# Attention before a mixture of experts: q, k and v in another layout in DRAM, and no transposes of q and k

## The chip, the cores and the metric

One core of one Trainium2 chip runs the whole program. The metric is the device time of one execution in microseconds (us); lower is better.

## The reference

Attention over 4 batches, 8 heads, 768 tokens and a head dimension of 64, in float32, and after it a mixture of 8 experts on the 3072 rows of 512 that it gives. A token sees the first 8 tokens and those up to 95 before it.

```python
scores = scale * np.matmul(q, k.transpose(0, 1, 3, 2))
keep = is_global | is_local            # global: pos < 8; local: 0 <= rel < 96
scores = np.where(keep, scores + bias, -1000000000.0)
a = np.exp(scores - np.max(scores, axis=-1, keepdims=True))
out = np.matmul(a / (np.sum(a, axis=-1, keepdims=True) + 1e-09), v)
x = out.transpose(0, 2, 1, 3).reshape(B * S, H * D)
...
logits = x @ w_gate
expert_idx = np.argmax(logits, axis=1)      # each token to one expert, by order of arrival
h = np.maximum(np.einsum('ecd,edf->ecf', disp, w1), 0.0)
y = np.einsum('ecf,efd->ecd', h, w2)
out[i] = gate_w[i] * y[expert_idx[i], pos[i]]
```

## The kernel before

The kernel has two stages. Attention (`banded`, line 560) goes through 24 blocks of 128 tokens, six to a batch; each block has two units of four heads, so there are 48 units. Behind it come the expert layers (from line 1042), 8 experts with 3 products of split float32 each.

A block goes through these steps, which the plan's jobs name:

- `load` (line 610): SyncE issues three DMAs, of q, k and v, each [128 tokens, 8 heads x 64] with one piece of 64 floats for each token and head.
- `turn` (line 648): 16 transposes on TensorE put the four head pairs of k and of q with the head dimension on rows into a pair of PSUM banks; `keep_qk` (line 658) copies them into the tile `K`, one half by VectorE, one by ScalarE (helper `keep_half`, line 194). A tile `K` serves two blocks and has two buffers.
- `keep_window` (line 666), once for two blocks, on GpSimd: copies of the last 96 keys of the block before and of the 8 global keys into the new tile.
- `scores` (line 687): 16 products for one unit, from the tile `K`. `maximum` (line 679) on VectorE adds the bias and takes the maximum, `exponential` (line 710) on ScalarE, `transpose_p` (line 727) on TensorE, `keep_p` (line 741) copies on VectorE and ScalarE, `weigh` (line 748) multiplies by v on TensorE. Three tiles `probs` hold the units' scores in turn.
- `load_window` (line 643): SyncE copies the last 96 rows of the block before from its tile `nat_v` in SBUF to a tile beside it; `load_globals` and `spread_globals` (lines 635 and 640) do so with the first 8 rows, once a batch.
- `keep_x`, `turn_x`, `scale_x`, `write_x`: the block's rows are turned back, scaled and written to DRAM (`xrows`). For every three blocks the routing steps (`zm` to `g`) and `write_slots` follow; some of them run on GpSimd.

Beside this, SyncE loads 12 pieces of 256 KB of the first expert's weights (job `weights`, tile `wst`, line 251), and GpSimd splits each into a high and a low part (`cast` at line 267, `split` at line 262).

The order of the work of all five engines in this stage is written out beforehand: the class `Plan` runs through the jobs with a cost each, and at each free moment of an engine takes the ready job with the least sum of its block number and its kind's number in `RANK`. The instructions are issued in that order; each engine, and SyncE's queue, works strictly in it. The setup of the bias (line 567) and the first loads stand ahead of the plan. `setup` makes `bias0` on VectorE (line 601) and `bias1` on GpSimd (line 603).

Of the kernel before, what the change touches and what calls it, by code (L numbers as in the profile page):

```python
# [12 lines left out]
F32 = mybir.dt.float32  # L13
# [9 lines left out]
P = 128  # L23
NEG = -1.0e9
FIXED = 4
FIRST = 2


class Plan:


    LATENCY = {"PE": 0.2, "ACT": 0.06, "DVE": 0.06, "POOL": 0.1, "SP": 2.1}
# [67 lines left out]
    def run(self, rank):  # L100
        for _, n in self.order(rank):
# [5 lines left out]
RANK = dict(landed=-8.58, load=-2.25, window=-0.06, globals=-0.01, spread=-0.22, turn=0.87, keep_qk=-1.73,  # L107
            keep_window=1.18, scores=-1.56, maximum=-0.47, exp=2.58, transpose_p=2.10, keep_p=1.46, weigh=3.45, sums=1.68,
            turn_sums=3.79, keep_x=2.05, turn_x=2.13, scale_x=2.07, write_x=2.06, zm=-1.83, za=2.95, lt=-0.50, ll=-0.09,
            m=0.12, f=3.81, np=-0.00, ne=5.82, nc=3.06, p=1.07, k=3.23, s=3.57, g=0.71, at=2.57, write_slots=-2.15,  # L110
            weights=1.88, cast=8.05, split=17.96, numbers=3.75, early=17.34, first=18.21, was_late=20.67,
            fetch_early=24.58, start_rows=19.45, turn_first=21.93, keep_high=22.50, keep_low=21.76, layer1_first=25.47,
            find_late=20.56, name_late=19.99, fetch_late=19.72)
# [3 lines left out]
def fused(ctx: ExitStack, tc, q, k, v, wg, w1, w2, out, n_global, n_local, cap):  # L117
    nc = tc.nc
    B, H, S, D = q.shape
# [7 lines left out]
    PREV, G = 96, 8  # L127
# [326 lines left out]
    def numbers(after=None):  # L454
        slot_i = small.tile([P, T4], I32, name="slot_i", bufs=1)
# [104 lines left out]
    def banded():  # L560
# [6 lines left out]
        def setup():  # L567

            rel_i = nat.tile([P, P], I32, name="rel_i", bufs=1)
            nc.gpsimd.iota(rel_i, pattern=[[-1, P]], base=0, channel_multiplier=1)  # L570
            rel0 = nat.tile([P, P], F32, name="rel0", bufs=1)
            nc.vector.tensor_copy(rel0, rel_i)
            rel1 = nat.tile([P, W], F32, name="rel1", bufs=1)
# [22 lines left out]
            near = nat.tile([P, HW], F32, name="near", bufs=1)  # L596
# [13 lines left out]
        def load(i, which="qkv"):  # L610

            b, j = blocks[i]
            d = st_[i]
            for n, src in zip("qkv", (q, k, v)):
                if n not in which:
                    continue
                d[n] = nat.tile([P, H * D], F32, name="nat_" + n, bufs=5 if n == "v" else 3)
                nc.sync.dma_start(out=d[n].rearrange("p (h d) -> p h d", h=H),  # L618
                                  in_=src[b, :, j * P:(j + 1) * P, :].rearrange("h p d -> p h d"))

        for which in ("qk", "v"):
            for i in range(2):
                load(i, which)
        setup()
        kpool = actx.enter_context(tc.tile_pool(name="kpool", bufs=2))
# [3 lines left out]
        probs = [soft.tile([P, HP + 4 * (HW + HP)], F32, name="sc", bufs=3) for _ in range(3)]  # L629
        for t in probs:  # L630
            nc.gpsimd.memset(t[:, 0:HP], 0.0)
            nc.gpsimd.memset(t[:, HP:].rearrange("p (a x) -> p a x", a=4)[:, :, HW:], 0.0)
        beside = [vpool.tile([PREV + G, H * D], F32, name="v1", bufs=3) for _ in range(3)]

        def load_globals(i):

            first["vg"] = vpool.tile([G, H * D], F32, name="vg")
            nc.sync.dma_start(out=first["vg"], in_=st_[i]["v"][0:G])

        def spread_globals(n):  # L640
            nc.sync.dma_start(out=beside[n][PREV:PREV + G], in_=first["vg"])

        def load_window(i):

            st_[i]["v1"] = beside[i % 3]
# [137 lines left out]
        for r in range(2):  # L783
            keep_qk(0, r)
# [640 lines left out]
```

## Time and profile before

| | us |
|---|---|
| median of 3 runs | 510.45 |
| lowest, highest | 509.27, 514.66 |
| the profiled execution | 513.04 |
| its span, first to last instruction | 511.2 |

The profile shows one execution. PE stands for TensorE's products, PEld for its loads of weights, DVE for VectorE, ACT for ScalarE, POOL for GpSimd, SP for SyncE, SPq for the issues on its queue. Products overlap each other on PE, so its busy time is that of their union, with ends that are modelled. The chain of work that ended last is followed back from the last instruction, at each step to what released it. A wait is put down to what came last of all that was waited for. Times on POOL are rough.

### The profile page before, as it was taken

To read this page: it belongs to the slowest core of one execution; us is meant where nothing else is said; L and a number is where in the kernel's file an instruction comes from. 1 tells how busy PE (TensorE), PEld (TensorE's weight loads), DVE (VectorE), ACT (ScalarE), POOL (GpSimd) and SP (SyncE) were. 2 spreads that over 40 slices of the span, in tenths; PEclk is the share of its full clock that TensorE was granted. 3 is DMA by queue.
4 is the path that set the end of the run, shared out by engine and by line. 5 is a ranking of instruction groups with operands and counts; after the bars stand their busy time and mean duration, and the time that the engine had idled before them with its cause. 6 is when DMAs were issued, how large, how long until landed. Compare 5 with 4: busy or idle time off the path is not lost.

```text
span 511.2 us, 12541 instructions
## 1 busy us (share of the span) xinstructions
PE 460.5 (90%) x4495; PEld 381.6 (75%) x4495; DVE 299.2 (59%) x925; ACT 295.0 (58%) x810; POOL 145.6 (28%) x265
## 2 busy tenths in 40 slices
PE   7799979878799779997999999999999999999780
PEld 4678757666577668786988999988989888988560
DVE  6588868767678652642664655645655554655430
ACT  4699877877797513343545555545555545555440
POOL 6022326654665412330311312121223103003011
PEclk9799999999998979998999999999999999999995
DMA  9899797879984317891653664554555355322001
GB/s 177 175 241 220 163 215 151 212 187 226 209 215 134 85 33 150 289 351 37 216 179 85 228 189 149 163 168 118 200 188 184 111 169 180 98 87 107 9 5 48
DMA packets 115815, 81.15 MB, mean 159 GB/s; under 512 B 81605, under 2 KB 98021, under 8 KB 115688
## 3 DMA queue, kind: packets, MB, share of 16 engines
q1 hardware_dynamic: 109112, 64.54, 48.4%
q0 software_dynamic: 5888, 14.71, 8.7%
q8 instruction: 96, 1.57, 1.3%
q14 instruction: 31, 0.25, 0.2%
q10 hardware_dynamic: 688, 0.07, 0.1%
HBM read 62.45 MB, written 14.75 MB: 151 GB/s over the span
## 4 chain that ended last, share of the span: by engine, by line
PE 50%; issue 27%; DMA 8%; POOL 5%; DVE 4%; SPq 2%; ACT 2%; POOLq 0%; ACTq 0%; DVEq 0%
PE bankC L554 16%; DMA nat_k<-in_k_dram 6%; PE y L1189 5%; PE y L1191 5%; PE y L1190 5%; PE pair L707 4%; PE pair L186 3%; PE pair L739 3%; PE bankC L765 3%; PE bankC L768 3%; POOL out_dram L1099 2%; DVE sc L682 1%; POOL xg L510 1%; PE bankC L491 1%; SPq L618 1%
## 5 line engine op out<-in xcount | busy, mean ns | idle before, releaser
L554 PE MATMUL bankC<-xh,w1h 128*128 128x416 f32 (+5 forms) x268 | 91.9, 348 | 3.8 <-ACT w2h L267 2.7
L1228 ACT ACTIVATE hh<-bankC 128x512 fp32r<-128x512 f32 (+1 forms) x67 | 38.8, 580 | 92.2 <-PE bankC L554 92.0
L554 PE MATMUL bankC<-xh,w1l 128*128 128x416 f32 (+5 forms) x268 | 90.5, 342 | 0.0
L1229 DVE SCALAR_TENSOR_TENSOR hl<-bankC,hh 128x512 fp32r<-128x512 f32 (+1 forms) x67 | 44.6, 667 | 75.0 <-ACT hh L1228 74.7
L716 ACT ACTIVATE sc<-sc,mx 128x168 f32<-128x168 f32 (+1 forms) x192 | 80.5, 423 | 4.2 <-DVE rs L725 2.8
L1189 PE MATMUL y<-w2h,hh 128*128 128x512 f32 x192 | 79.0, 411 | 0.7 <-ACT hh L1228 0.7
L1191 PE MATMUL y<-w2h,hl 128*128 128x512 f32 x192 | 75.9, 395 | 0.0
L1190 PE MATMUL y<-w2l,hh 128*128 128x512 f32 x192 | 75.8, 395 | 0.0
L554 PEld LDWEIGHTS bankC<-xh,w1h 128*128 128x128 f32 x268 | 51.9, 194 | 12.4 <-issue 4.7
L510 POOL DMA_INDIRECT xg<-xrows,gi x28 | 28.5, 1018 | 112.2 <-PE bankC L491 98.1
L554 PE MATMUL bankC<-xl,w1h 128*128 128x416 f32 (+5 forms) x268 | 58.0, 338 | 0.0
L682 DVE CUSTOM_DVE_ANT_0 sc<-pair,bias 128x168 f32<-128x168 f32 (+1 forms) x192 | 51.4, 321 | 10.6 <-PE pair L707 9.2
L554 PEld LDWEIGHTS bankC<-xh,w1l 128*128 128x128 f32 x268 | 52.0, 194 | 3.1 <-issue 0.4
L270 DVE TENSOR_TENSOR w1l<-wr,w1h 128x512 fp32r<-128x512 f32 x58 | 37.5, 689 | 27.8 <-ACT w1h L267 27.8
L1231 ACT ACTIVATE hr<-bankC 128x256 f32<-128x256 f32 x64 | 24.6, 385 | 49.5 <-DVE hl L1229 49.5
L1099 POOL DMA_INDIRECT out_dram<-ysb,to x16 | 16.0, 998 | 128.1 <-ACT ysb L1091 125.7
L270 DVE TENSOR_TENSOR w2l<-w2r,w2h 128x512 fp32r<-128x512 f32 x58 | 37.5, 688 | 19.2 <-ACT w2h L267 19.2
L554 PEld LDWEIGHTS bankC<-xl,w1h 128*128 128x128 f32 x268 | 47.7, 191 | 0.7
L1189 PEld LDWEIGHTS y<-w2h,hh 128*128 128x128 f32 x192 | 36.2, 189 | 10.9 <-issue 4.2
L1191 PEld LDWEIGHTS y<-w2h,hl 128*128 128x128 f32 x192 | 36.0, 188 | 8.6
L707 PE MATMUL pair<-K 64*64 64x168 f32 (+1 forms) x768 | 37.8, 313 | 3.9 <-DVE K L194 1.8
L1190 PEld LDWEIGHTS y<-w2l,hh 128*128 128x128 f32 x192 | 36.3, 189 | 5.9
(188 smaller groups left out, 803.9 us busy)
## 6 DMA issues: line engine op xcount, KB each, us to landing
wr<-in_moe_w_dram SPq DMA_DIRECT2D x58, 256.0 KB
w2r<-in_moe_w_dram SPq DMA_DIRECT2D x58, 256.0 KB
nat_q<-in_q_dram SPq DMA_DIRECT2D x24, 256.0 KB
nat_k<-in_k_dram SPq DMA_DIRECT2D x24, 256.0 KB
nat_v<-in_v_dram SPq DMA_DIRECT2D x24, 256.0 KB
xrows<-xr SPq DMA_DIRECT2D x23, 256.0 KB
v<-nat_v SPq DMA_DIRECT2D x20, 192.0 KB
wst<-in_moe_w_dram SPq DMA_DIRECT2D x12, 256.0 KB
```

Source lines behind the costliest of these rows:

```text
L270: (nc.gpsimd if meanwhile else nc.vector).tensor_tensor(parts["l"][:, s], r, parts["h"].bitcast(F32)[:, s], op=ALU.subtract)
L510: ld = nc.gpsimd.indirect_dma_start(out=xg, out_offset=None, in_=xrows[0:n], in_offset=bass.IndirectOffsetOnAxis(ap=gi.bitcast(U32), axis= ...
L554: nc.tensor.matmul(h_ps[:, s], ww[:, c, fs], xx[:, c, s], start=n == 0, stop=n == 3 * KC - 1)
L682: x = nc.vector.tensor_tensor_reduce(out=un["sc"][:, a, 0:un["w"]], in0=un["ps"][hh][:, gg, :], in1=un["bias"][:, 4 * (u % 2) + a, :], sca ...
L707: nc.tensor.matmul(pss[hh][r * HP:(r + 1) * HP, gg, :], kq[rows, 1, g, q0:q0 + HP], kq[rows, 0, g, k0:k0 + w], start=True, stop=True)
L716: nc.scalar.activation(sc[:, a, 0:w], sc[:, a, 0:w], AF.Exp, bias=un["mx"][:, a:a + 1], scale=-1.0, accum_out=st_[i]["sm"][:, 4 * half + a ...
L1099: w = nc.gpsimd.indirect_dma_start(out=out, out_offset=bass.IndirectOffsetOnAxis(ap=rows.bitcast(U32)[:, 0:1], axis=0), in_=ysb, in_offset ...
L1189: nc.tensor.matmul(y, hh[:, t], w2h[:, fi], start=f == 0, stop=False)
L1190: nc.tensor.matmul(y, hh[:, t], w2l[:, fi], start=False, stop=False)
L1191: nc.tensor.matmul(y, hl[:, t], w2h[:, fi], start=False, stop=f == NF - 1)
L1228: nc.scalar.activation(hh[:, s], h[:, s], AF.Relu)
L1229: nc.vector.scalar_tensor_tensor(hl[:, s], h[:, s], 0.0, hh.bitcast(F32)[:, s], op0=ALU.max, op1=ALU.subtract)
```

## The change

The host gives q and k as [batch, block, 128 rows of two heads x 64, 4 head pairs, 128 tokens], and v as [batch, token, 512]. The DMAs of k go straight into the tile `K` (now without q, and with four buffers), those of q into a tile of its own (five buffers); `turn` and `keep_qk` are gone, and `scores` reads both tiles. v has six buffers; its windows and global rows come from DRAM. The setup of the bias uses the third tile `probs` as its room. The 12 weight pieces are asked for later, from unit 28 on. The numbers in `RANK` and the plan's delay of a DMA are new, so the order of all engines in attention is another one; the expert layers are written as before.

```diff
-    LATENCY = {"PE": 0.2, "ACT": 0.06, "DVE": 0.06, "POOL": 0.1, "SP": 2.1}
+    LATENCY = {"PE": 0.2, "ACT": 0.06, "DVE": 0.06, "POOL": 0.1, "SP": 2.6}
...
-RANK = dict(landed=-8.58, load=-2.25, window=-0.06, globals=-0.01, spread=-0.22, turn=0.87, keep_qk=-1.73,
-            keep_window=1.18, scores=-1.56, maximum=-0.47, exp=2.58, transpose_p=2.10, keep_p=1.46, weigh=3.45, sums=1.68,
...
+RANK = dict(landed=-8.58, load=-4.46, window=-2.20, spread=-0.53, keep_window=1.49, scores=-1.56, maximum=0.58, exp=1.41,
+            transpose_p=2.10, keep_p=-0.67, weigh=2.64, sums=1.68, turn_sums=3.86, keep_x=1.25, turn_x=1.84, scale_x=2.79,
+            write_x=2.99, zm=-1.83, za=2.84, lt=-0.50, ll=-0.40, m=0.21, f=3.54, np=0.36, ne=3.48, nc=1.82, p=1.07,
+            k=3.47, s=3.57, g=0.71, at=3.23, write_slots=-3.66, weights=1.84, cast=8.05, split=17.96, numbers=3.75,
...
-        def setup():
-
-            rel_i = nat.tile([P, P], I32, name="rel_i", bufs=1)
+        def setup(spare):
+
+            rel_i, rel0, rel1, near = [spare[:, o:o + n] for o, n in ((0, P), (P, P), (2 * P, W), (2 * P + W, HW))]
+            rel_i = rel_i.bitcast(I32)
...
-        def load(i, which="qkv"):
-
+        kpool = actx.enter_context(tc.tile_pool(name="kpool", bufs=2))
+        KT, KB, QB, VB = 2, 4, 5, 6
+
+        def load_q(i):
             b, j = blocks[i]
-            d = st_[i]
-            for n, src in zip("qkv", (q, k, v)):
-                if n not in which:
-                    continue
-                d[n] = nat.tile([P, H * D], F32, name="nat_" + n, bufs=5 if n == "v" else 3)
-                nc.sync.dma_start(out=d[n].rearrange("p (h d) -> p h d", h=H),
-                                  in_=src[b, :, j * P:(j + 1) * P, :].rearrange("h p d -> p h d"))
-
-        for which in ("qk", "v"):
-            for i in range(2):
-                load(i, which)
-        setup()
+            st_[i]["q"] = nat.tile([P, NP, P], F32, name="q", bufs=QB)
+            nc.sync.dma_start(out=st_[i]["q"], in_=q[b, j])
+
+        def load_v(i):
+            b, j = blocks[i]
+            st_[i]["v"] = nat.tile([P, H * D], F32, name="v", bufs=VB)
+            nc.sync.dma_start(out=st_[i]["v"], in_=v[b, j * P:(j + 1) * P, :])
+
+        def load_k(i, which=range(2)):
+            b, j = blocks[i]
+            if i // KT not in keys:
+                keys[i // KT] = kpool.tile([P, NP, KT * KS + PREV], F32, name="K", bufs=KB)
+            for s in which:
+                o = s * KS + PREV + G
+                ld = nc.sync.dma_start(out=keys[i // KT][:, :, o:o + P], in_=k[b, j + s])
+            return ld
+
+        load_k(0, [0])
+        load_q(0)
+        apart_k = load_k(0, [1])
+        load_q(1)
+        load_v(0)
+        load_v(1)
...
+        setup(probs[2])
...
-        def load_globals(i):
-
-            first["vg"] = vpool.tile([G, H * D], F32, name="vg")
-            nc.sync.dma_start(out=first["vg"], in_=st_[i]["v"][0:G])
-
-        def spread_globals(n):
-            nc.sync.dma_start(out=beside[n][PREV:PREV + G], in_=first["vg"])
+        def spread_globals(b, n):
+            nc.sync.dma_start(out=beside[n][PREV:PREV + G], in_=v[b, 0:G, :])
...
-            nc.sync.dma_start(out=beside[i % 3][0:PREV], in_=st_[i - 1]["v"][P - PREV:P])
-
-        def turn(i):
-
-            ps = st_[i]["qk"] = pair()
-            for m, n in enumerate(("k", "q")):
-                for g in range(NP):
-                    last = turn_halves(ps, g + NP * m, st_[i][n][:, g * P:(g + 1) * P])
-            return last
...
-            keep_half(r, both[:, :, s * KS + PREV + G:(s + 1) * KS + PREV], st_[i]["qk"], 2 * NP)
+            nc.sync.dma_start(out=beside[i % 3][0:PREV], in_=v[b, j * P - PREV:j * P, :])
...
-                        nc.tensor.matmul(pss[hh][r * HP:(r + 1) * HP, gg, :], kq[rows, 1, g, q0:q0 + HP],
-                                         kq[rows, 0, g, k0:k0 + w], start=True, stop=True)
+                        q0 = r * HP
+                        made = nc.tensor.matmul(pss[hh][r * HP:(r + 1) * HP, gg, :], st_[i]["q"][rows, g, q0:q0 + HP],
+                                                kq[rows, g, k0:k0 + w], start=True, stop=True)
...
-        turn(0)
         busy(6)
-        for r in range(2):
-            keep_qk(0, r)
...
+                job("load", (t, "q"), "SP", 0.9, lambda t=t: load_q(t), [("scores", 2 * (t - QB) + 1)])
+                job("load", (t, "v"), "SP", 0.9, lambda t=t: load_v(t), [("load", (t, "q")), ("weigh", 2 * (t - VB) + 1)])
+                if t % KT == 0:
+                    job("load", (t, "k"), "SP", 2.2, lambda t=t: load_k(t),
+                        [("load", (t - 1, "q")), ("scores", 2 * (t - KT * KB) + 3), ("keep_window", t - KT * (KB - 1))])
...
+                job("window", t, "SP", 0.75, lambda t=t: load_window(t), [("weigh", 2 * (t - 3) + 1), ("maximum", (0, 3))])
...
-                job("keep_window", t, "POOL", 0.5, lambda t=t: keep_window(t), [("keep_qk", (n, r)) for n in (t, t - 1) for r in (0, 1)])
+                job("keep_window", t, "POOL", 0.5, lambda t=t: keep_window(t), [("load", (t, "k")), ("load", (t - KT, "k"))])
...
-            job("weights", n, "SP", 0.75, loads[n], [("maximum", (2 * (n + 10), 0)), ("split", n - 4)])
-            job("cast", n, "POOL", 0.63, lambda n=n: splits[n](meanwhile=True, which=(0,)), [("weights", n), ("maximum", (2 * (n + 11), 0))])
+            job("weights", n, "SP", 0.75, loads[n], [("maximum", (min(2 * (n + 14), n + 34), 0)), ("split", n - 4)])
+            job("cast", n, "POOL", 0.63, lambda n=n: splits[n](meanwhile=True, which=(0,)), [("weights", n)])
...
+def laid_out(name, a, n_global, n_local):
+
+    if name not in "qkv" or not is_banded(n_global, n_local):
+        return a
+    B, H, S, D = a.shape
+    if name == "v":
+        return a.transpose(0, 2, 1, 3).reshape(B, S, H * D)
+    return a.reshape(B, H // 2, 2, S // P, P, D).transpose(0, 3, 2, 5, 1, 4).reshape(B, S // P, 2 * D, H // 2, P)
```

## Rows read from the trace of the kernel before

**Rows 1.** the page: an engine's busy us, share, instructions; DMA packets by size

```profile
PE 460.5 (90%) x4495; PEld 381.6 (75%) x4495; DVE 299.2 (59%) x925; ACT 295.0 (58%) x810; POOL 145.6 (28%) x265
...
DMA packets 115815, 81.15 MB, mean 159 GB/s; under 512 B 81605, under 2 KB 98021, under 8 KB 115688
```

**Rows 2.** stretches: start:end, us, busy us (instructions) by engine, clock, DMA share, GB/s

```profile
7.40:179.20 171.80, 147.95 (x2855) 116.05 (x2855) 130.12 (x602) 135.56 (x497) 73.86 (x166) 0.97 0.83 187
14.20:21.05 6.85, 4.73 (x64) 4.31 (x64) 1.39 (x2) 3.17 (x11) 0.00 (x0) 0.50 0.96 193
21.05:45.00 23.95, 23.84 (x493) 19.18 (x491) 20.17 (x92) 22.16 (x80) 5.06 (x23) 1.00 1.02 224
21.05:154.20 133.15, 117.07 (x2339) 91.69 (x2339) 104.75 (x481) 109.52 (x401) 59.67 (x140) 1.00 0.90 203
154.20:157.60 3.40, 3.40 (x44) 2.75 (x43) 2.57 (x14) 2.26 (x9) 3.14 (x6) 0.50 0.78 216
...
100.00:179.20 79.20, 66.19 (x1239) 51.48 (x1237) 58.78 (x269) 59.34 (x215) 42.59 (x81) 0.97 0.76 177
```

**Rows 3.** PE's waits from 7 to 179 us: us in total, times, longest

```profile
PE pair L186 <- DMA nat_k<-in_k_dram: 12.3, 5, 3.6
PE pair L491 <- DMA xge<-xrows,gie: 2.6, 1, 2.6
```

**Rows 4.** the chain that ended last, 130 to 182 us: start, us, what

```profile
132.04 6.21 DMA nat_k<-in_k_dram
...
138.38 0.72 PE pair L186 x16
...
144.56 0.66 PE pair L186 x16
```

**Rows 5.** timeline: start, us, engine, line, operation; idle before it and releaser

```profile
4.87 1.64 DVE L601 TENSOR_SCALAR bias<-rel 128x128 f32<-128x128 f32 x8 [1.22 <-POOL rel L585]
...
7.40 1.10 PE L707 MATMUL pair<-K 64*64 64x128 f32 x32 [0.88 <-DVE K L194]
...
8.13 0.29 DVE L682 CUSTOM_DVE_ANT_0 sc<-pair,bias 128x128 f32<-128x128 f32 x1 [0.87 <-PE pair L707]
...
16.32 0.69 PE L186 MATMUL pair<-ident,nat_k 64*128 64x64 f32 x8 [3.58 <-DMA nat_k<-in_k_dram]
...
138.38 0.47 PE L186 MATMUL pair<-ident,nat_k 64*128 64x64 f32 x8 [2.69 <-DMA nat_k<-in_k_dram]
...
154.03 1.04 PE L739 MATMUL pair<-ident,sc 64*128 64x64 f32 x16 [1.65 <-DVE K L194]
```

**Rows 6.** groups to 200 us by line, shape: busy us, mean ns, idle before

```profile
L194 DVE COPY K<-pair 128x512 f32<-128x512 f32 x24 | 16.5, 686 | 14.1 <-PE pair L186 13.9
...
L194 ACT COPY K<-pair 128x512 f32<-128x512 f32 x24 | 14.1, 587 | 15.1 <-PE pair L186 14.6
```

**Rows 7.** a stretch of the expert layers, columns as in rows 2

```profile
300.00:400.00 100.00, 100.00 (x515) 88.37 (x515) 55.30 (x86) 55.75 (x110) 22.14 (x22) 1.00 0.55 174
```

**Rows 8.** SyncE's issues at line 618: ns min/median/max, first and last start

```profile
L618 SPq DMA_DIRECT2D nat_k<-in_k_dram x24: 375/614/3412, 1.3 to 150.8; - x24
```

**Rows 9.** weight pieces, then those from 100 us: ns min/median/max, first, last start

```profile
L251 SPq DMA_DIRECT2D wst<-in_moe_w_dram x12: 377/433/1327, 72.2 to 147.5; - x12
...
L267 POOL CAST w1h<-wst x6: 609/610/613, 77.5 to 143.1; 128x512 fp32r<-128x512 f32 x6
...
L262 POOL TENSOR_TENSOR w1l<-wst,w1h x6: 1269/1275/1279, 78.2 to 143.8; 128x512 fp32r<-128x512 f32 x6
...
L251 SPq DMA_DIRECT2D wst<-in_moe_w_dram x8: 377/566/1327, 100.5 to 147.5; - x8
```

**Rows 10.** the same chain as in rows 4, at 148 to 155 us

```profile
148.80 1.25 POOL w2l L262
...
153.28 0.61 DVE K L194
```

**Rows 11.** waits from 15 to 200 us: us in total, times, longest

```profile
POOL xg L510 <- DVE hl L1229: 12.9, 1, 12.9
```

More of the change, by code (lines that the diff above doesn't have):

```diff
@@ L454, in numbers @@
     def numbers(after=None):
-        slot_i = small.tile([P, T4], I32, name="slot_i", bufs=1)
+        start_rows()
+        slot_i = rt.tile([P, DM], F32, name="xge", bufs=FIRST).bitcast(I32)[:, 0:T4]
         x = nc.gpsimd.iota(slot_i, pattern=[[1, T4]], base=0, channel_multiplier=0)
@@ L705, in scores @@
                         k0 = o + PREV + G if j == 0 else o + r * HP
-                        q0 = o + PREV + G + r * HP
-                        nc.tensor.matmul(pss[hh][r * HP:(r + 1) * HP, gg, :], kq[rows, 1, g, q0:q0 + HP],
-                                         kq[rows, 0, g, k0:k0 + w], start=True, stop=True)
+                        q0 = r * HP
+                        made = nc.tensor.matmul(pss[hh][r * HP:(r + 1) * HP, gg, :], st_[i]["q"][rows, g, q0:q0 + HP],
+                                                kq[rows, g, k0:k0 + w], start=True, stop=True)
+                        if i == 0:
+                            tc.declare_no_dep(made.ins, apart_k.ins, reason="the second block has columns of its own")
         def exponential(u, a):
@@ L810, in banded @@
-            if t > 0:
-                if t == 1:
-                    job("landed", t, "SP", 1.0, lambda: None, late=0.0)
-                job("turn", t, "PE", 0.5, lambda t=t: turn(t), [("load", (t, "q")), ("load", (t, "k")), ("landed", t)], takes="pair")
-                for r, e in enumerate(("DVE", "ACT")):
-                    job("keep_qk", (t, r), e, (0.69, 0.59)[r], lambda t=t, r=r: keep_qk(t, r),
-                        [("turn", t)] + [("scores", 2 * (t - n) + 1) for n in range(2, 5)] + [("keep_window", t - 2)],
-                        frees=("turn", t))
+                    job("spread", (t, n), "SP", 0.25, lambda b=b, n=n: spread_globals(b, n),
+                        [("weigh", 2 * (t - m) + 1) for m in range(1, 4)] + [("maximum", (0, 3))])
+            else:
+                job("window", t, "SP", 0.75, lambda t=t: load_window(t), [("weigh", 2 * (t - 3) + 1), ("maximum", (0, 3))])
@@ L895, in banded @@
         job("was_late", 0, "DVE", 0.15, was_late, [("first", 0)])
-        job("start_rows", 0, "ACT", 0.0, start_rows, [("fetch_early", 0)])
         for a in range(FIRST):
-            job("turn_first", a, "PE", 0.45, lambda a=a: turn_first(a, bankP([P, KC, P])), [("start_rows", 0)], takes="pair")
+            job("turn_first", a, "PE", 0.45, lambda a=a: turn_first(a, bankP([P, KC, P])), [("fetch_early", 0), ("numbers", 0)], takes="pair")
             job("keep_high", a, "ACT", 0.6, lambda a=a: keep_high(a), [("turn_first", a)])
```

50 lines of the change are left out of this document (17 added, 33 removed).

## The prediction

> **What bounds the kernel now.** I read the page's busy shares first, then the stretch of attention by itself, then who waits in it. The page says 90% TensorE (PE) and that most DMA packets are small [rows 1]. One stretch of 171.8 us, from the first scores to the last copy of weighted values, is the only place the change touches. In it PE is busy 147.95 us, ScalarE (ACT) 135.56, VectorE (DVE) 130.12, GpSimd (POOL) 73.86, and the DMA engines 0.83 of the time [rows 2]. The rest of the span, the expert layers, keeps its work: the 332 us behind 179.2 I take as moved, not changed.
>
> Within the stretch PE sets the pace. From 21.05 to 45 us it is busy 23.84 of 23.95 us, although ACT is busy 22.16 beside it [rows 2]: that is how tightly this plan runs when nothing is late. What is late is input. PE's longest waits by far are for a landing `nat_k`, 12.3 us in five waits [rows 3], and the chain shows what such a wait looks like: 6.21 us of DMA, and PE's transposes only behind it [rows 4]. One more wait is of interest, 2.6 us for the early rows; it stays.
>
> One of the five waits, 3.58 us at 16.32, has a sequel [rows 5]. From 14.20 to 21.05 the granted clock is 0.50, that is 1.2 GHz in place of 2.4 [rows 2], after PE had stood idle since about 12.7.
>
> **The change, part by part.** *Transposes of K and Q on PE.* A block's 16 transposes take 0.66 to 0.72 us of the chain [rows 4]; I take 0.69. Block 0's lie ahead of the stretch, so 23 x 0.69 = 15.9 us leave the engine that sets the pace. Bounds 15.2 and 16.6.
>
> *Their copies out of PSUM.* 24 copies of 16.5 us in all leave DVE and 14.1 us leave ACT [rows 6]. ACT falls to about 121.5 and DVE to 113.6, PE to about 132. PE stays the busiest, so I count these copies at nothing; what covers them is PE's own work, and without that cover (an engine already first) they would be worth 14 to 16 us instead of the transposes, not in addition.
>
> *The loads.* Before, 72 loads of q, k and v run in pieces of 64 floats, 256 bytes: 72 x 1024 = 73,728 of the 81,605 packets under 512 bytes [rows 1]. After, Q and V are 2 KB per partition, and K lands in pieces of 512 bytes. The stretch moves about 32 MB by the code: q, k, v and the written rows 25.2, the windows of v 3.9, weights 3.1. Before, the queues gave 203 GB/s at a share of 0.90, or 226 GB/s full [rows 2]; when weights alone are loaded, in pieces of 1 and 2 KB, 174 at 0.55, or 316 [rows 7]. So the DMA work is 32/226 = 143 us now and 102 us at the better rate. K's pieces lie between both rows: at the worse one 26/316 + 6.3/226 = 110 us. I take 110, as nothing here moves 512-byte pieces. In a stretch of some 146 us that is a share of 0.75, and Q is asked for five blocks ahead and K four pairs ahead, instead of three blocks. So I take out all five waits, 12.3 us; bounds 8.7 (if the first one only changes its name) and 12.3. The Trainium skill, "DMA: Bandwidth & Descriptors", Specifications, puts the smallest transfer that reaches line rate at 512 bytes; by it K's pieces cost no more than Q's, the DMA work would be 102 us, and the second rival below would deserve about half its chance. No row shows such a piece, so sum and chances are made without it.
>
> *The low clock behind the first wait.* 4.73 us of PE work were done there at half clock [rows 2], worth 2.4 us at full clock. Without the idle time ahead of it I take 2.4; bounds 0 and 2.4. The later spell at 154.20 (3.40 us, so 1.7 us) I leave standing.
>
> *The start.* Block 0's scores begin at 7.40, after transposes and copies; then the first maximum starts at 8.13. But the bias must be there, and DVE makes it until 4.87 + 1.64 = 6.51 [rows 5]. So at most 1.6 us; below, nothing, if the tables that now share the third probability tile are made later. I take 1.0.
>
> *SyncE's order.* Per block it issues as many transfers as before: q, v, one of a K pair's two on average, a window and a written row, against q, k, v, window, row. The copy of the global rows (`vg`, 4 times) goes, and the windows come from DRAM and wait for no `nat_v`. Issues lasted up to 3.41 us for `nat_k` while the DMA engines were full [rows 8]; with a lower share they should shorten. Counted at nothing: hidden by the depth of the buffers. If that cover fails, the second rival holds.
>
> *Weights later, on POOL.* The 12 weight pieces are asked for from unit 28 of 48 on, not 20; each costs POOL 0.61 + 1.275 = 1.89 us [rows 9]. In the last 79.2 us before, POOL was busy 42.59, with 8 of the 12 pieces in it [rows 2, 9]. The same 22 units should take 66 us, with all 12: 42.6 + 7.6 = 50 us, 75% where it was 54%. POOL carries steps of the routing, so DVE and then PE can wait for it. The chain shows one such case: a split of 1.25 us, then routing steps on POOL, DVE's late copy, and PE after it [rows 10]; PE waited 1.65 us there [rows 5].
>
> *What is given back.* Without `nat_k`, PE idles 133.15 - 117.07 - 8.7 = 7.4 us between 21.05 and 154.20 [rows 2, 3]; 8.7 are the four later waits. These stay, since I subtracted only the waits on input. But waits on input also let ACT, DVE and POOL catch up. Their shares of a shorter stretch rise (ACT from 0.79 to 0.83, POOL to 0.75 at the end), so I add 6 us of new waits, nearly as much again. Bounds: 0, as in the stretch at 99.5%, and 15.3, twelve splits of 1.275 us each ahead of a routing step that PE comes to wait for.
>
> **The sum.** 15.9 + 12.3 + 2.4 + 1.0 = 31.6, less 6 is 25.6 us. The profiled execution took 513.04 us (span 511.2), 2.6 above the median of the three runs, 510.45. The terms are differences, so I take them off the median: 484.9 us. With nothing given back 478.9; with the second low spell and the 2.6 us wait for early rows gone too, 474.6.
>
> **Rivals.** *POOL takes PE's place at the end of the stretch* (give-back of 15.3, gain 16.3): 494 us. For it: 75% of POOL and the chain just named. Against: the splits stand last in the order by their rank (17.96), and POOL stood idle 12.9 us before the late rows are fetched, room for six of them [rows 11].
>
> *The slower one: K comes too late.* A pair's tile has one wait for two transfers, and POOL's `keep_window` waits for it with the routing steps queued behind; scores wait for `keep_window`. SyncE goes in order, so a row or weight piece that waits holds a K pair back. If each of the 11 later pairs costs PE w, the gain is 25.6 - 11w: gone at w = 2.3, slower by 1% from w = 2.8; at w = 3.5 it is 12.9 us slower, 523 us. For it: waits of this size are in the trace (3.58, four others averaging 2.2), and a DMA of 6.21 us to land [rows 4, 5]. Against: eight blocks of K in flight, and a DMA share that falls.
>
> *A low clock over much of the stretch.* PE has less to do and might be granted 1.2 GHz longer. Each us of low clock costs 0.5 us, so the gain is gone after 51 more us of it; over half of the 146 us, 36 us are lost, 521 us. Against: 10.25 us of 171.8 were low, after idle time, and idle time should shrink. And a wait of 2.69 us that ended at 138.38 was followed by work at full clock [rows 2, 5]. The Trainium skill, "TensorE: Matmul & The Clock Gate", Part 1, has the lower state as the default that activity lifts; the trace agrees at 14.20, and by that rule alone, with work taken from PE, I would give this rival more than 0.03.
>
> **How the numbers follow.** Forecast 0.66; POOL 0.17; K late, in any size, 0.07; low clock 0.03; more than forecast (under 478) 0.07. The likeliest gives 485. Between 477 and 499 lie the forecast, the POOL case and a part of the last one, leaving out about 2 in 10. About 1% is what a measurement of this kernel can tell from no change: faster by more than that, the forecast, POOL and the greater gains whole and a little of the K case, 0.91; within 1%, over half of the K case and a third of the low clock, 0.05; slower, the rest of both, 0.04.
>
> **What would show it.** Stage: from first scores to last weighted value about 146 us, PE busy about 132 of it. Input: PE's waits on a DMA in it near nothing, and a DMA share of 0.70 to 0.78 there. Start: block 0's scores before 6.5 us, and no low clock between 14 and 21. Give-back: the waits of PE for DVE and of DVE for POOL after unit 28; over 15 us of them is the POOL rival. K late: waits on `K<-in_k_dram`. I am wrong altogether if the part behind the last weighted value, some 332 us, grows.

## The result, and the profile after

The changed kernel takes 490.55 us (median of 4 runs, 484.26 to 494.77) against 511.91 of the kernel before beside it, a ratio of 0.954 [0.943, 0.966]. Run twice more, each time with the kernel before beside it, it took 484.73 (0.951 [0.947, 0.956]) and 487.42 us (0.955 [0.946, 0.964]). A ratio leaves out executions that were clearly slower than the fastest of their kernel, so it is not quite the quotient of the medians shown. Forecast were 485, in a range of 477 to 499.

| | before | changed, first profile | second | third |
|---|---|---|---|---|
| profiled execution, us | 513.04 | 490.04 | 483.90 | 487.77 |
| its span | 511.2 | 488.3 | 482.1 | 486.0 |
| first scores to last copy of weighted values | 171.80 | 148.19 | 141.60 | 147.70 |
| the rest behind it | 332.0 | 333.9 | 334.9 | 331.2 |

The span's difference lies in the stretch that the change touches: 23.6, 30.2 and 24.1 us less. Behind it are 1.9 and 2.9 us more, and 0.8 less. Of the page of the first profile these lines, on the engines and the packets, answer to [rows 1]:

```profile
PE 450.0 (92%) x4111; PEld 368.5 (75%) x4111; DVE 283.4 (58%) x901; ACT 281.6 (58%) x786; POOL 145.7 (30%) x265
...
DMA packets 60451, 81.03 MB, mean 166 GB/s; under 512 B 7845, under 2 KB 36549, under 8 KB 60328
```

The 384 transposes of K and Q are gone from PE (4495 to 4111), and 73,760 packets below 512 bytes are gone from the queues. Next the stretches of the first profile, with the columns of [rows 2]: the whole stage, a low clock at its start, the plain part behind it, and a low clock at its end.

```profile
6.26:154.45 148.19, 134.59 (x2480) 103.13 (x2479) 114.20 (x576) 121.56 (x472) 74.99 (x170) 0.97 0.85 217
12.09:18.91 6.82, 6.50 (x78) 5.09 (x79) 2.88 (x17) 5.19 (x22) 1.04 (x4) 0.50 0.98 251
18.91:45.00 26.09, 26.09 (x515) 20.50 (x515) 21.66 (x104) 23.92 (x90) 5.50 (x25) 1.00 0.78 232
152.03:158.86 6.83, 6.37 (x43) 5.55 (x44) 3.90 (x21) 2.02 (x5) 0.00 (x0) 0.50 0.06 5
```

The second profile, in its stage and in the same stretch of the start, shows no low clock there:

```profile
5.60:147.20 141.60, 130.43 (x2479) 100.19 (x2478) 115.38 (x579) 122.28 (x472) 74.55 (x170) 1.00 0.85 225
...
12.09:18.91 6.82, 6.06 (x128) 4.99 (x128) 5.08 (x27) 6.67 (x29) 1.04 (x4) 1.00 0.99 269
```

PE's waits in the second profile's stage (total, times, longest), where [rows 3] had 12.3 us on `nat_k`:

```profile
PE pair L189 <- DVE pay L426: 1.6, 2, 0.9
PE bankC L759 <- DVE oh L371: 1.6, 1, 1.6
...
PE pair L699 <- DMA q<-in_q_dram: 0.8, 1, 0.8
```

One wait on a DMA is left, 0.8 us. PE's idle time is now made of many small waits for DVE, ACT and POOL.

One thing in the first and third profiles is odd. The timeline of the third, at the last unit's transposes of the probabilities (idle time before, and what ended it, in brackets):

```profile
147.46 0.44 PE L339 MATMUL pair<-ident,z 128*128 128x128 f32 x2
...
147.83 0.71 PE L733 MATMUL pair<-ident,sc 64*128 64x64 f32 x16
...
148.99 0.39 DVE L345 TENSOR_TENSOR lh<-pair,rs_last 128x128 f32<-128x128 f32 x1 [1.61 <-PE pair L733]
...
151.94 0.59 ACT L197 COPY pt<-pair 128x512 f32<-128x512 f32 x1 [4.82 <-remote]
151.96 0.69 DVE L197 COPY pt<-pair 128x512 f32<-128x512 f32 x1 [1.56 <-remote]
...
152.80 0.69 PE L759 MATMUL bankC<-pt,v 104*64 104x128 f32 x4 [4.25 <-DVE oh L371]
```

By their records the transposes end at 148.54. The copies that wait for them start at 151.94, released by something that the view calls remote. The semaphore that PE raises when it is done was raised 3.55 us after the last of these transposes had begun (3.74 in the first profile). In the second the same copies start at 144.57 and 145.21, behind transposes that began at 143.76. Then PE waited 1.6 us, not 4.3. The matmuls ahead of the transposes (L339) are late too: VectorE's step that reads them starts 1.53 us after they began (1.62 in the first profile), and 0.47 us in the second. So whatever it is sets in before the transposes.

### The profile page after: what moved, and what is told of

The parts are those of the page before. It is cut to its first block, busy times and chain, and to the rows that moved or that the text cites. A ratio compares the mean times of both kernels' runs of the same rounds, so it can differ in the third digit from the quotient of the medians.

```text
span 488.3 us, 11722 instructions
## 1 busy us (share of the span) xinstructions
PE 450.0 (92%) x4111; PEld 368.5 (75%) x4111; DVE 283.4 (58%) x901; ACT 281.6 (58%) x786; POOL 145.7 (30%) x265
## 4 chain that ended last, share of the span: by engine, by line
issue 54%; POOL 10%; PE 5%; DVE 2%; POOLq 0%; another core or an unknown queue 0%; ACT 0%; DVEq 0%
POOL xg L514 5%; POOL out_dram L1082 4%; PE pair L733 1%; PE bankC L759 1%; PE bankC L558 1%; PE bankC L762 1%; POOL table L436 1%; DVE pt L197 0%; PE pair L495 0%; PE pair L189 0%; PE pair L699 0%; POOLq L514 0%; DVE sc L674 0%; POOLq L1082 0%
## 5 line engine op out<-in xcount | busy, mean ns | idle before, releaser
L558 PE MATMUL bankC<-xh,w1l 128*128 128x416 f32 (+5 forms) x268 | 89.5, 339 | 0.0
L514 POOL DMA_INDIRECT xg<-xrows,gi x28 | 28.5, 1018 | 113.2 <-PE bankC L495 98.9
L699 PE MATMUL pair<-K,q 64*64 64x168 f32 (+1 forms) x768 | 38.1, 316 | 2.5 <-ACT xt L768 0.6
```

What stands on the lines that cost most here:

```text
L514: ld = nc.gpsimd.indirect_dma_start(out=xg, out_offset=None, in_=xrows[0:n], in_offset=bass.IndirectOffsetOnAxis(ap=gi.bitcast(U32), axis= ...
L558: nc.tensor.matmul(h_ps[:, s], ww[:, c, fs], xx[:, c, s], start=n == 0, stop=n == 3 * KC - 1)
L699: made = nc.tensor.matmul(pss[hh][r * HP:(r + 1) * HP, gg, :], st_[i]["q"][rows, g, q0:q0 + HP], kq[rows, g, k0:k0 + w], start=True, stop= ...
```

## Experiments

A measure that runs through them is the pace of the 24 blocks: from the first to the last copy of weighted values by ScalarE (first and last start in the view of its line), which leaves the kernel's start and its end out. Before, the second profile of the changed kernel, and, as they are told below, long rows alone, transposes alone, transposes with copies, copies alone (each bank with one reader), and small pieces of q and v:

```profile
L774 ACT COPY xt<-bankC x24: 564/586/588, 20.2 to 179.2; 128x512 f32<-128x512 f32 x24
```
```profile
L768 ACT COPY xt<-bankC x24: 563/586/592, 16.2 to 147.2; 128x512 f32<-128x512 f32 x24
```
```profile
L773 ACT COPY xt<-bankC x24: 562/585/589, 17.6 to 167.4; 128x512 f32<-128x512 f32 x24
```
```profile
L775 ACT COPY xt<-bankC x24: 560/586/592, 17.0 to 158.5; 128x512 f32<-128x512 f32 x24
```
```profile
L780 ACT COPY xt<-bankC x24: 562/586/589, 18.0 to 167.8; 128x512 f32<-128x512 f32 x24
```
```profile
L768 ACT COPY xt<-bankC x24: 565/585/592, 18.3 to 156.6; 128x512 f32<-128x512 f32 x24
```
```profile
L769 ACT COPY xt<-bankC x24: 563/585/593, 18.3 to 168.6; 128x512 f32<-128x512 f32 x24
```

| kernel | time, us | ratio to before | pace, us | rest behind, us |
|---|---|---|---|---|
| before | 510.17 | | 159.0 | 332.0 |
| before, with long rows | 500.95 | 0.981 [0.977, 0.985] | 149.8 | 333.2 |
| changed, with transposes and copies | 507.32 | 1.001 [0.996, 1.006] | 149.8 | 337.7 |
| changed, with transposes | 500.16 | 0.982 [0.977, 0.987] | 141.5 | 338.8 |
| changed, with copies, one reader a bank | 504.42 | 0.989 [0.981, 0.997] | 138.3 | 341.3 |
| changed, q and v in 256 bytes | 502.82 | 0.984 [0.974, 0.993] | 150.3 | 332.3 |
| changed, three times | 490.55, 484.73, 487.42 | 0.951 to 0.955 | 136.4, 131.0, 136.5 | 333.9, 334.9, 331.2 |

Times are medians; pace and rest are those of the profiled execution. Before was taken anew beside each set, at 509.48 to 511.91 us, and the ratios go by that; the time shown for it is that of the first set. The order of a kernel is planned by its job costs, so a kernel with added jobs has an order of its own. That limits what a run here can say. Of each edit the body is shown; the jobs and ranks that put it into the plan are left out. By its medians the kernel with transposes and copies would stand at 0.994, not 1.001; either way it shows no gain over the kernel before.

**The changed kernel again.**

> The changed kernel unaltered, timed and profiled once more. Theory (the completion of unit 47's transposes that was reported 3.5 us late, at 148 to 151.5 us, is an accident of one execution): no gap of over 2 us on TensorE between 140 and 156 us, stage about 144 to 146 us, time 484 to 488. Rival (it belongs to this order of work): the gap of 4.4 us before L759 is there again at about 152 us, stage about 148, time 489 to 492. Either way the low clock at about 12 to 19 us should be there again if thin activity of TensorE ahead of it is the reason.

Measured: 484.73, no gap of 4 us, a stage of 141.6 us; the low clock of 12 to 19 us was not there, though the order was the same. A third time, beside the last runs:

> The changed kernel unaltered, on the same chip as the three runs beside it, as their measure. It took 490.6 and 484.7 us (medians) on two chips. 484 to 491.

Measured: 487.42, with the late report of PE again (4.25 us). So it is no accident of one execution, since two of three profiles have it at this one place, and no necessity of the order either. PE's wait there is long in the two runs with early weights too (2.5 us) and in the two with small pieces (4.3 and 3.6). What holds PE there is open: no view names it. It matters for what follows: of the 5.5 us of pace between the second profile and the other two some 2.7 can be this wait (4.4 and 4.3 us against 1.6), and the second alone has no low clock in its pace. Low clock at the start: 6.8, 0 and 3.4 us in the three. In the first profile PE works in small pieces there, with short gaps in which it waits for GpSimd and for ScalarE's exponentials:

```profile
11.30 0.65 PE L733 MATMUL pair<-ident,sc 64*128 64x64 f32 x4 [0.19 <-POOL sm L714]
12.36 1.22 PE L733 MATMUL pair<-ident,sc 64*128 64x64 f32 x12 [0.41 <-ACT sc L710]
```

The second profile has the same two gaps, at full clock, so they don't decide it:

```profile
10.77 0.65 PE L733 MATMUL pair<-ident,sc 64*128 64x64 f32 x4 [0.19 <-POOL sm L714]
11.82 0.95 PE L733 MATMUL pair<-ident,sc 64*128 64x64 f32 x12 [0.41 <-ACT sc L710]
```

**The transposes put back.** Added to the changed kernel, for blocks 1 to 23:

```
+        def turn(i):
+            ps = st_[i]["qk"] = pair()
+            for m in range(2):
+                for g in range(NP):
+                    turn_halves(ps, g + NP * m, st_[i]["q"][:, g])
```

> The changed kernel plus 16 transposes of 64x64 per block (of its Q tile, into PSUM that nobody reads), 23 blocks, the number that the change removed; loads as in the changed kernel, no copies. The order is planned anew with them. Theory (TensorE sets the pace, so a transpose costs what it lasts): 23 x 0.69 = 15.9 us more than the changed kernel, 500 to 507. Rival (TensorE had room, the gain came from the loads alone): within 4 us of the changed kernel, 486 to 494. Kernel before: 510 to 512.

Measured: 500.16, that is 15.4 above the changed kernel on the same chip, where 15.9 were forecast. The rival, that the loads alone carried the gain, falls. Not all of it is pace, though: 10.5 us against the second profile (neither has the late report; 3.4 us of this run's pace were at low clock), and 3.9 us lie behind the last weighted values. There PE waits 3.4 us for the early rows (1.8 in the second profile), and the clock is low for longer. The 40 us behind the last weighted values, with the columns of [rows 2], in the second and third profile of the changed kernel, and with transposes, with transposes and copies, and with copies alone (one reader a bank):

```profile
147.20:187.20 40.00, 33.10 (x194) 27.46 (x193) 19.95 (x83) 11.79 (x26) 11.24 (x11) 0.91 0.55 163
```
```profile
154.80:194.80 40.00, 36.18 (x205) 30.14 (x206) 19.90 (x82) 11.82 (x26) 10.19 (x10) 0.88 0.58 170
```
```profile
158.50:198.50 40.00, 29.00 (x168) 24.48 (x169) 16.08 (x74) 9.32 (x23) 9.19 (x9) 0.83 0.47 125
```
```profile
167.80:207.80 40.00, 29.67 (x167) 24.72 (x166) 14.46 (x63) 8.36 (x19) 8.70 (x10) 0.79 0.44 111
```
```profile
156.60:196.60 40.00, 28.27 (x167) 23.78 (x168) 15.70 (x66) 8.98 (x20) 10.12 (x12) 0.74 0.45 111
```

The three runs whose rest grew have a mean clock of 0.83, 0.79 and 0.74 there, against 0.91 and 0.88. How much of a longer rest is the wait and how much the clock is not shown apart.

**Transposes and copies.** As before, and their PSUM tile is copied out, a half each by DVE and ACT, into a tile that nobody reads:

```
+        def keep_qk(i, r):
+            keep_half(r, spare, st_[i]["qk"], 2 * NP)
```

> As the run with the extra transposes, and their results copied out of PSUM too, one half by VectorE (0.69 us) and one by ScalarE (0.59 us) per block, into a tile that nobody reads: the work of the kernel before under the loads of the changed one. Theory (copies counted at nothing, TensorE covers them): within 3 us of the run with the transposes alone, and 10 to 14 us faster than the kernel before (the waits on input and what else the loads bring), 497 to 502 if the terms of the sum hold. Rival (copies cost as much as the transposes, 14 to 16 us, because ScalarE and VectorE are bounds in turn): 512 or more.

Measured: 507.32, 7.2 us above the transposes alone, neither 3 nor 15; in pace 8.3 us (6.8 us of low clock in it, 3.4 in the other). The copies were not free. Its pace equals that of the kernel before with long rows, 149.8 us, told next, which does the same work per block: the new ranks, the deeper buffers and the later weights show no gain in pace of their own here. It loses 4.5 us to that one behind the last weighted values.

**Long rows alone.** The kernel before, with one edit besides the host's layout:

```
-                nc.sync.dma_start(out=d[n].rearrange("p (h d) -> p h d", h=H),
-                                  in_=src[b, :, j * P:(j + 1) * P, :].rearrange("h p d -> p h d"))
+                nc.sync.dma_start(out=d[n], in_=src[b, j * P:(j + 1) * P, :])
```

> The kernel before with one edit: q, k and v are laid out by tokens on the host, so each load moves 2 KB per partition in place of eight pieces of 256 bytes; transposes, copies, windows and order stay. Theory (five waits on nat_k, 12.3 us, come from small pieces, and the rest of the gain from the transposes): 496 to 501, a ratio of 0.972 to 0.982, hardly a wait on nat_k left, DMA share of the stretch about 0.75. Rival 1 (the pieces alone carry the whole gain): 486 to 493. Rival 2 (the loads are asked for too late, the pieces don't matter): 508 to 512, the waits on nat_k stay.

Measured: 500.95, ratio 0.981, inside what the theory gave as a ratio, at its edge as a time. PE's waits on `nat_k` fell from 12.3 us [rows 3] to this:

```profile
PE pair L186 <- DMA nat_k<-in_k_dram: 0.6, 1, 0.6
```

So the pieces made these waits, and long rows, which took them away, were worth 9.2 us, in time as in pace. Rivals 1 and 2 fall.

**Small pieces in the changed kernel.** First all of q, k and v, K's in four transfers a block, from a layout with the halves of 64 tokens apart:

```
-                ld = nc.sync.dma_start(out=keys[i // KT][:, :, o:o + P], in_=k[b, j + s])
+                for g in range(NP):
+                    ld = nc.sync.dma_start(out=keys[i // KT][:, g, o:o + P].rearrange("p (r t) -> p r t", r=2),
+                                           in_=k[b, j + s, 2 * g:2 * g + 2].rearrange("r p t -> p r t"))
```

> The changed kernel with q, k and v read from DRAM in pieces of 256 bytes (64 floats) as before the change: the host lays out q and k so that no piece is longer, v is read by heads; the windows of v stay rows. A block of K takes four transfers in place of one. No transposes, no copies, same buffers. Theory (pieces make the waits on input; at 226 GB/s the stretch's 32 MB need 143 us of the DMA engines, as long as the whole stretch): DMA share 0.95 or more, waits of TensorE on K, q or v of 8 to 15 us, time 493 to 502. Rival (it is the asking ahead, five blocks of Q and eight of K, that took the waits away, not the pieces): 484 to 488, hardly a wait on a DMA.

Measured: 525.2, above both. But its DMA share was 0.78, not 0.95, and PE waited 18.9 us for v: it seems that not the DMA engines were full, but SyncE was late. Its issues last 144.5 us of the 187 us stage when added up over the timeline, 61 of them for K's 88 transfers. The granted clock of the stage fell to 0.88 as well. So the run says little of pieces. Then q and v alone, with as many transfers as in the changed kernel:

```
-            nc.sync.dma_start(out=st_[i]["q"], in_=q[b, j])
+            nc.sync.dma_start(out=st_[i]["q"].rearrange("p g (r t) -> p (g r) t", r=2), in_=q[b, j].rearrange("x p t -> p x t"))
...
-            nc.sync.dma_start(out=st_[i]["v"], in_=v[b, j * P:(j + 1) * P, :])
+            nc.sync.dma_start(out=st_[i]["v"].rearrange("p (h d) -> p h d", h=H), in_=vh[b, :, j * P:(j + 1) * P, :].rearrange("h p d -> p h d"))
```

> The changed kernel with q and v alone read from DRAM in pieces of 256 bytes, K in its pieces of 512; as many transfers as in the changed kernel (in the earlier run K took four times as many, and SyncE issued for 144.5 of 187 us). Theory (small pieces cost by the time that they take from SyncE and the DMA engines, and a share near 0.9 brings waits back): issuing on SyncE 85 to 110 us of the stretch, DMA share 0.88 or more, 4 to 12 us above the changed kernel beside it. Rival 1 (the depth of the buffers hides it): within 2 us of it. Rival 2 (the earlier run's 525 us came from the small pieces themselves, not from its extra transfers): 25 us or more above it.

Measured: 502.82, 15.4 us above the changed kernel beside it, more than the theory and less than the second rival. The theory's signs are there: a DMA share of 0.92 in the stage, some 125 us of issues (more than it said), and a wait of PE on a DMA, one of 5.3 us. The granted clock of the stage is 0.94, where the changed kernel beside it has 0.97, so some of the 15.4 us is clock; the parts are not shown apart. What a full DMA does to SyncE is seen on the write of a row, whose own form is the same everywhere (256 KB in rows of 2 KB; ns min/median/max of one issue). Before, third profile of the changed kernel, then small pieces of q and v:

```profile
L307 SPq DMA_DIRECT2D xrows<-xr x23: 350/538/2947, 24.8 to 172.1; - x23
```
```profile
L310 SPq DMA_DIRECT2D xrows<-xr x23: 343/379/1391, 28.7 to 147.4; - x23
```
```profile
L311 SPq DMA_DIRECT2D xrows<-xr x23: 343/1342/3597, 32.5 to 162.1; - x23
```

The same issue takes 538, 379 or 1342 ns (medians), depending on what else is on its way; from about 20 to 130 us the DMA share is 0.90, 0.89 and 1.02 in the three. All issues together last 128.7 us of the kernel before's stage, 74.6 of the changed one's first profile and 82.3 with long rows alone, each summed over the timeline, to within about 1 us.

**Copies alone.** In the first form both engines copied the weighted values' bank:

```
+        def copy_x(i, r):
+            (nc.vector.tensor_copy, nc.scalar.copy)[r](spare[:, r], st_[i]["xt_ps"])
```

> The changed kernel plus, per block, a copy of 128x512 out of PSUM by VectorE (0.69 us) and one by ScalarE (0.59 us), from the weighted values into a tile that nobody reads: the copies that the change removed, without the transposes. The order is planned anew. The run with transposes and copies stood 7.2 us above the one with transposes alone, so the copies are in doubt. Theory (they hide behind TensorE's work, as the prediction counted them): 483 to 488. Rival 1 (they cost 7 us because VectorE and ScalarE feed TensorE closely): 490 to 494. Rival 2 (ScalarE becomes the bound and its 14.1 us come whole): 497 or more.

Measured: 505.49, beyond all three. Here ScalarE's copy of the weighted values came behind VectorE's copy of the same bank (14 times, with 12.7 us of idle time before them), an order that the kernel before did not have:

```profile
60.85 0.69 DVE L773 COPY spare_x<-bankC 128x512 f32<-128x512 f32 x1 [1.01 <-PE bankC L762]
...
61.58 0.59 ACT L768 COPY xt<-bankC 128x512 f32<-128x512 f32 x1 [2.95 <-DVE spare_x L773]
```

Of the 2.95 us in this row the first 2.2 went by before VectorE's copy could start either; being second cost 0.73 us. So the run prices these waits along with the copies. In the second form each bank has one reader:

```
+        def copy_v(i):
+            nc.vector.tensor_copy(spare[0].rearrange("p (r x) -> p r x", r=2), rows_ps[i][:, :, 0:KC * HP])
+        def copy_a(i):
+            nc.scalar.copy(spare[1].rearrange("p (c t) -> p c t", c=KC), st_[i]["xt_ps"])
```

> The changed kernel plus, per block, a copy of 128x512 out of PSUM by VectorE (of the turned rows, ahead of their scaling, which VectorE does too) and one by ScalarE (of the weighted values, behind the copy that ScalarE makes of them anyway), into tiles that nobody reads. In the earlier run with copies alone VectorE and ScalarE read one bank of PSUM, and the one waited for the other (ScalarE 2.95 us at 61.6); here each bank has one reader. Theory (VectorE and ScalarE have so little room that copies cost part of their 16.5 and 14.1 us even without the transposes): 5 to 10 us above the changed kernel beside it. Rival 1 (copies hide, and the earlier run's 20 us were its waits of one reader for the other): within 2 us of it. Rival 2 (they come whole): 14 us or more above it.

Measured: 504.42, 17.0 above the changed kernel beside it, as the second rival said. But the profile puts it elsewhere than that rival did. It is of the fastest of the four executions, 499.68 us, so it shows only 11.9 of the 17.0. The pace is 138.3 us, 1.8 above the third profile's. That one has the late report and 4.4 us of low clock in its pace, however, and this run has neither, as its last unit shows:

```profile
155.48 0.44 PE L759 MATMUL bankC<-pt,v 104*64 104x128 f32 x4 [1.58 <-DVE pt L197]
```

Like for like is the second profile, 131.0 us, on another chip: 7.3 us, near the 8.3 that the copies cost on top of the transposes. The rest behind it is 341.3 us in place of 331.2. PE waited there for the early rows, since POOL, which fetches them, had stood 6.61 us before an earlier scatter of its queue:

```profile
PE pair L495 <- DMA xge<-xrows,gie: 8.4, 1, 8.4
```
```profile
158.92 0.97 POOL L436 DMA_INDIRECT table<-pay,slot_of  x1 [6.61 <-DMA xrows<-xr]
159.96 0.24 POOL L490 TENSOR_SCALAR gie<-tbe 128x2 int32<-128x2 int32 x1
160.48 1.10 POOL L514 DMA_INDIRECT xge<-xrows,gie  x1 [0.28 <-POOL gie L490]
```

In the third profile the fetch is issued at 146.16, 8.65 us ahead of the last weighted copy at 154.81; here 3.9 us behind it. A good part of the 17 us is this hand-over, with the longer low clock shown above, in an order planned anew, and not the copies' work on the blocks.

**Weights early.** The one edit:

```
-            job("weights", n, "SP", 0.75, loads[n], [("maximum", (min(2 * (n + 14), n + 34), 0)), ("split", n - 4)])
+            job("weights", n, "SP", 0.75, loads[n], [("maximum", (2 * (n + 10), 0)), ("split", n - 4)])
```

> The changed kernel with one edit: the weight pieces may be asked for from unit 20 on, two units apart, as before the change, in place of unit 28 on, a unit apart; POOL's casts and splits of them come earlier with them. Theory (POOL's later and denser work at the end costs nothing that shows): 483 to 487, and the time from the last weighted value's copy to the end stays at 334 to 335 us. Rival 1 (POOL delays the routing at the end of attention, and with it the early rows): 480 to 482, that time 332 to 333 us. Rival 2 (weights earlier collide with the loads of q, k and v): 487 to 490, with waits of TensorE on a DMA.

Measured: 491.85, but the changed kernel was not beside it. So once more with it:

> The changed kernel with the weight pieces asked for from unit 20 on, two units apart, once more, with the changed kernel beside it. Theory (when POOL does the weights makes no difference that shows): within 2 us of the changed kernel. Rival 1 (later weights cost, by POOL's load at the end of attention): 2 to 5 us below it. Rival 2 (later weights are worth something, since earlier ones collide with loads or with routing): 3 to 8 us above it.

Measured: 492.38, 5.0 us above the changed kernel (490.78 to 494.01 against 485.03 to 490.62). Weights later are worth something; that POOL's load at the end costs is the rival that falls. The pace is the same (136.6 and 136.5 us). In the profiles 3.0 us lie behind the last weighted values (334.2 against 331.2), but the unchanged kernel's own three profiles span 331.2 to 334.9 there. So where the 5.0 us lie is not shown, and what early weights collide with was not tried.

**Matmuls against the low clock.** Extra matmuls on a constant, overwritten before anybody reads them, at the start and around the end of attention:

```
+    def fill(ps, n):
+        for _ in range(n):
+            nc.tensor.matmul(ps.rearrange("p (c t) -> p c t", t=P), warm,
+                             warm.unsqueeze(1).to_broadcast([P, ps.shape[1] // P, P]), start=True, stop=True)
...
+        if a == 0:
+            fill(ps.rearrange("p c t -> p (c t)"), 6)
         turn_rows(ps, first["rows"][a])
```

> The changed kernel plus matmuls on a constant whose results are overwritten before anybody reads them, where TensorE waits: ahead of the transposes of the first four units (two of 256 columns per four of them), and ahead of five steps around the end of attention (before the last weighted values 10 of 256 columns, before the early rows' transposes 6 of 512, 4 each before the last count and the last step of finding the late rows). The order of all else stays. Theory (thin activity of TensorE at these places lets the granted clock fall to 0.50 in some executions, 3.4 or 6.8 us at a time): no low clock before 20 us, and about one spell of 3.4 us less between 140 and 175 us, time 481 to 484. Rival 1 (low clock does not depend on it): the same spells, 484 to 487. Rival 2 (the extra matmuls delay what they stand before): 487 to 490.

Measured: 493.18, ratio 0.967 [0.961, 0.972]: not faster, and by the ratios about 1% above the changed kernel. The start did keep its full clock, and still the first copy of weighted values came at 19.3 us, later than in any of the three profiles of the changed kernel (18.0, 16.2, 18.3). At the start the matmuls cost more than the clock they saved. The changed kernel was not beside this run.

## Why the prediction was right, step by step

**Transposes, 15.9 us.** Right in time, 15.4 when put back, but not all of it as forecast: 10.5 are pace, the rest lies behind the last weighted values and at the start. PE's busy time in the stage fell by 13.4, 17.5 and 15.4 us in the three profiles.

**Copies, at nothing.** Wrong as an addition. On top of the transposes they cost 7.2 us, 8.3 in pace, and without them 7.3 us of pace against the second profile. "PE stays the busiest" was true and not enough: with transposes and copies ACT is busy 134.1 us, DVE 128.2 and PE 146.8 in a stage of 162.3, and each block goes through all three in turn. From "transposes and copies" to neither, on one chip, is 507.3 to 484.7, that is 22.6 us, where the sum had 15.9. How much of it is work and how much the order is not settled, as each kernel has its own.

**Loads, 12.3 us.** Right in kind, some 3 us too large: the waits went (12.3 to 0.6 us) and gave 9.2 us with long rows alone. The forecast that DMA share falls to 0.70 to 0.78 was wrong; it was 0.85, 0.85 and 0.82, and 0.83 before. So in the changed kernel it was not more room on the DMA engines that took the waits away; which it was, fewer pieces, shorter issues or loads asked for earlier, is not shown apart. With long rows alone the share did fall, to 0.73.

The step that failed in the forecast of the share is the rate of 2 KB rows, taken from the expert layers [rows 7]; their stretch holds gathers and scatters in 4 KB packets too (1201 of them from 300 to 400 us before), so it is not of weights alone, as I had it. With reads, windows and written rows mixed, 217 GB/s at 0.85 is 255 GB/s full (198 at 0.73, or 271, with long rows alone), not the 291 of 32 MB in 110 us. In the packets of 19 to 120 us of the first profile a 2 KB packet takes 126 ns of an engine on average (16 engines at that make 260 GB/s), one of 512 bytes 28.5 ns (287 GB/s; 123 and 32.2 ns in the third profile), one of 256 bytes before the change 20.4 ns (201 GB/s). K's pieces are thus about as good as rows in this mix, and the lower rate that I chose for them was not needed. The Trainium skill, "DMA: Bandwidth & Descriptors", Specifications, has 512 bytes as the smallest transfer at line rate; these packets agree in that, while the 102 us of DMA work that I worked out by it came to 126 (0.85 of 148.19).

**SyncE, at nothing.** The issues did shorten, from 128.7 to 74.6 us, but not by the mechanism named, a lower DMA share: that did not fall. What that is worth in time was not tried by itself.

**The low clock at the start, 2.4 us, and the start, 1.0.** Half right. The spell was there in two of three profiles (6.8, 3.4 us, and none), without a long wait ahead of it, so it was not the wait on `nat_k` alone that made it. Together the two terms were 3.4 us; the first weighted copy came 2.2, 4.0 and 1.9 us earlier than the 20.2 of before. The scores of block 0 began at 6.26, 5.57 and 7.10, not always before 6.5.

**Given back, 6 us.** Near in size: PE stands idle 13.6, 11.2 and 15.1 us in the stage, where the forecast's stage of 146 us with 132 of work had 14. In part this is luck, as 4.4 and 4.3 us of the idle time in the first and third profile are the wait behind PE's late report, which no step had. POOL was not the bound. It was busy 49.47 us of the last 70.45 in the first profile, as forecast, and weights earlier made the kernel slower. But DVE waited longer for it: 7.9, 7.8 and 4.8 us in the last 67 to 71 us of the stage, 3.3 in the last 79 before; how much of that reached PE is not shown.

**The rest behind.** It was to stay 332 us, and it was 331.2 to 334.9. But in three experiments it grew to 337.7 to 341.3, with an early-rows fetch that came late (waits of 3.4, 4.2 and 8.4 us) and more low clock. That hand-over sits next to the end of the stage. I knew the wait, 2.6 us [rows 3], and no rival of mine let it grow.

The sum came out at 25.6 us, and 21 to 25 were measured. Its parts did not come out like that. In pace, from the kernel before to the second profile, long rows gave 9.2 us, the copies 8.3 and the transposes 10.5, that is 28.0, each from one profile and with an order of its own; the sum had 12.3, 0 and 15.9, that is 28.2. That what it put too high and what it put at nothing cancel is luck. In the other two profiles the pace is 5.4 and 5.5 us longer, with low clock and PE's late report in it. No rival took place: PE did not wait on K, and POOL did not become the bound. For the low clock the Trainium skill, "TensorE: Matmul & The Clock Gate", Part 1, has a default that activity lifts. The trace agrees before the change, where the spell at 14.20 came with 3.58 us of idle time; on the spell at 12.09 it decides nothing, as the second profile ran the same order with the same gaps at full clock.

## What to carry to other kernels

Where three engines hand a block to one another and each is busy for over three quarters of the time, don't price one engine's work at nothing because another is busier: the copies here were worth 7 to 8 us of pace. Look at the hand-over behind the stage too: what is fetched for the next stage must be issued before the last block, or a part of what the pace gains is lost there. And when an experiment replans an order, compare the pace of the blocks and the rest separately, profile the unchanged kernel more than once, and compare with the profile that had the same accidents.

## What the runs showed of the hardware

- PE's semaphore for a group of transposes came up 3.55 and 3.74 us after the last one had begun, in two profiles of three; the copies waiting for it stood still until then. The matmuls before them were reported late too. The cause is open.
- The same order had low clock for 6.8, 0 and 3.4 us at its start, with the same gaps on PE ahead of it. In the first profile 6.50 us of matmul work were done in 6.82 us at 0.50.
- An issue of the same write takes SyncE 379 ns (median) at a DMA share of 0.89, and 1342 ns at 1.02, where q and v move in 256-byte pieces.
- Rows and K's pieces under mixed load moved at some 255 GB/s full (217 at a share of 0.85), where the expert layers had 316 [rows 7].
